# Readers of a PSUM tile in a fixed order, ScalarE alone on two kinds of shared tile, and every engine's order made anew

## The chip, the cores and the metric

The kernel runs on one core of a Trainium2 chip. The time is the device time of one launch in microseconds (us); shown is the median of several runs. The engines of the core: TensorE (PE, its weight loads are PEld), VectorE (DVE), ScalarE (ACT), GpSimd (POOL) and SyncE (SP). PE writes only into PSUM, eight banks here; DVE and ACT read PSUM and SBUF. DMA transfers are issued by SP, by POOL where they accumulate, and a few by ACT.

## The reference

The input x is 2048 x 512 in float32. One branch filters it with a two-dimensional Fourier transform, the other is a dense layer of 512 to 1792 to 512 with gelu, and a gate per row mixes them:

```python
X = jnp.fft.rfft2(x, axes=(-2, -1))
a = jnp.fft.irfft2(X * (w_r + 1j * w_i), s=(S, D), axes=(-2, -1))
h = _gelu(jnp.einsum("bsd,df->bsf", x, w1) + b1)
b = jnp.einsum("bsf,fd->bsd", h, w2) + b2
g = _sigmoid((x * gate_w).sum(-1, keepdims=True))
return g * a + (1 - g) * b
```

## The kernel before

**Arithmetic.** Products that need full precision are made of two parts per operand, a high part `h` (a copy into the fast fp32r format) and a low part `l` (the difference), and three matmuls: high by high, high by low, low by high. So nearly every result in PSUM is followed by an ACT copy (`copy`, L418) for the high part and a DVE subtraction (L460) for the low part.

**The Fourier branch.** `forward(j)` is done for 16 groups of 128 rows. PE folds the columns into two PSUM banks `pd` (one for the cosine part, one for the sine part; the gate's logit stands in two columns between). ACT copies each into the high part of `zb` (L601), DVE subtracts into its low part (L604), ACT takes the logit's two columns (L605): three reads of one PSUM tile by two engines. A second product goes to `py`: ACT copies it after its first half into `pys[0]` and again at its end into `Y[j][0]` (L622), DVE makes `pys[1]` of the two (L623), and ACT puts that into `Y[j][1]` by halves (L626). Then come radix-4 stages on DVE, the multiplication by the filter (`wf`, loaded through SP, L745 to L758), and `inverse(c, h)` eight times: products into `pz`, copied and subtracted into `zb` (L807, L808), products into `pa`; of `pa`, `od` is an ACT copy at half time, `u` an ACT copy at the end (L832), `v` = `pa` - 2 `od` on DVE (L833), and four sums and differences on DVE, two of `pa` and `u`, two of `v` (L837).

**The dense branch.** x stands in four column blocks. `CA` are the first two (done first), `CB` the last two. `seven` multiplies two blocks of x by two blocks of weights in seven products instead of eight, in the PSUM banks `nu` and `ux`; what it needs of the weights are seven tiles, `0h 0l sh sl th tl 1`, made once from `w1` for `CA` and stored to DRAM (`su<-wA..`, L1046), and loaded again for `CB` (`wB..<-su`, L406). Some tiles of `w2` go to DRAM the same way (`sb..`, L875, and `wb..b<-sb`). Other low parts come from an accumulating DMA on POOL (L403): ACT writes the negative of the high part (L465), and the DMA adds the full weight from DRAM. `gelu` works in PSUM (L878), `g_..h` is the high part of the activations (L418) and `g_..l` the low part (L460). `down` sums over four groups of rows of `w2` in `po` banks: ACT first puts the running sum `s` into the bank (L927), the matmuls add onto it, ACT takes it out again (L418).

**The end.** The blocks of `CA` leave `s` as `bacc` in DRAM (L943); the Fourier result adds it by a POOL accumulation (`w<-bacc`) and leaves by `out<-w` (L843). The blocks of `CB` are mixed in `last`: DVE makes `t` from `po` and the gate `gb` (L957), subtracts it from the Fourier result `y` (L966), and SP stores it (`out<-t`, L972; the very last piece goes by ACT, L970).

**What sets the order.** Each piece of work is a step (`add`) with an engine, a cost, a lag, and the buffers that it reads and writes. A planner, which isn't part of the file, made from these a list of step numbers, `ORDER`, and a list of buffer places, `SLOTS`. The kernel emits its steps in the order of `ORDER`, so each engine and each queue gets its instructions in that sequence and does them strictly one behind the other. Every tile has one fixed place (`slots`); where two tiles share a place, the later one waits until the earlier one's last reader is done, be it a store. These waits come from the framework, which also makes two engines take turns at one PSUM tile.

Of the kernel before, what the change touches and what calls it, by code (L numbers as in the profile page):

```python
# [16 lines left out]
P = 128  # L17
# [248 lines left out]
class Step:  # L266
    def __init__(self, n, eng, cost, lag, emit, bufs):
        self.n, self.eng, self.cost, self.lag, self.emit, self.bufs = n, eng, cost, lag, emit, bufs
        self.after = []
        self.need = 0  # L270

        self.table = None


class Graph:
# [4 lines left out]
    def add(self, eng, cost, lag, emit, reads=(), writes=()):  # L280
# [12 lines left out]
        for x in reads:  # L293
            b, ps = parts(x)
            for p in ps:
                if b.wrote[p] is not None:
                    deps.add(b.wrote[p])
# [927 lines left out]
```

## Time and profile before

| what | value |
|---|---|
| median of 3 runs | 390.59 us (389.73 to 391.59) |
| the profiled execution | 390.88 us |
| its span | 389.1 us |
| mean granted PE clock | 0.982 |
| PE busy | 362.3 us, 1782 matmuls |
| PEld busy | 299.5 us |
| DVE busy | 324.6 us, 672 instructions |
| ACT busy | 299.8 us, 614 instructions |
| POOL busy | 40.5 us |
| moved by DMA | 69.85 MB, mean 179 GB/s |

Times in the profile are us from the span's start. PE's waits are what matters most: an engine that PE never waits for may idle at no cost. SPq is SP's queue, in which transfers are issued one after the other; a transfer that waits there for its buffer holds up all behind it. A row of waits names the waiting engine, the tile it was about to write, and then what it waited for. "Granted clock" is the share of the full clock that PE got.

### The profile page before, as it was taken

What the parts mean: (1) busy time and instruction counts of PE and PEld (TensorE: products, weight loads), DVE (VectorE), ACT (ScalarE), POOL (GpSimd) and SP (SyncE); (2) the same over time, 40 slices, a digit from 0 to 9 for tenths busy, and PEclk for the clock granted to TensorE, in tenths of its full rate; (3) what the DMA queues carried; (4) which work ended last, traced back from release to release, by engine and by line L of the source; (5) the groups of instructions that cost most, each with busy time, mean ns of one, the idle gap of its engine ahead of it and who ended that gap; (6) DMA issues with size and microseconds to landing.
All of it is one profiled execution on the core that took longest, in us unless ns stands there. A gap on an engine that the chain in (4) does not pass through costs nothing. (4 is left out here: it accounts for less than half of the span.)

```text
span 389.1 us, 5714 instructions
## 1 busy us (share of the span) xinstructions
PE 362.3 (93%) x1782; PEld 299.5 (77%) x1782; DVE 324.6 (83%) x672; ACT 299.8 (77%) x614; POOL 40.5 (10%) x54
## 2 busy tenths in 40 slices
PE   7999899998897999987999999889999999999993
PEld 5977788786676788866878888668877887887882
DVE  4978698999878999969899999958789867496873
ACT  3788889889987976747867778959999998978510
POOL 1200001000104000110000002000000010111340
PEclk9899999999999999998999999989999999999997
DMA  8998385556669958795795895622123238454588
GB/s 274 326 257 288 79 219 108 141 172 210 152 205 240 275 189 259 255 224 171 223 338 151 226 293 144 144 73 71 16 54 98 91 63 266 115 89 115 135 174 259
DMA packets 46350, 69.85 MB, mean 179 GB/s; under 512 B 5488, under 2 KB 19312, under 8 KB 46320
## 3 DMA queue, kind: packets, MB, share of 16 engines
q1 hardware_dynamic: 38752, 58.36, 45.0%
q0 software_dynamic: 7136, 10.79, 18.5%
q8 instruction: 14, 0.23, 0.3%
q10 hardware_dynamic: 432, 0.33, 0.3%
q14 instruction: 16, 0.13, 0.1%
HBM read 51.76 MB, written 17.57 MB: 178 GB/s over the span
## 5 line engine op out<-in xcount | busy, mean ns | idle before, releaser
L927 ACT ACTIVATE po<-s 128x512 f32<-128x512 f32 (+1 forms) x49 | 28.6, 588 | 3.5 <-DVE t L957 3.1
L418 ACT ACTIVATE s<-po 128x512 f32<-128x512 f32 x40 | 23.4, 592 | 4.3 <-PE po L409 4.1
L788 ACT ACTIVATE sw<-y,al 64x512 f32<-64x512 f32 x32 | 23.0, 720 | 2.0 <-DVE y L654 1.5
L409 PE MATMUL py<-zb,tf 128*128 128x258 f32 x96 | 20.1, 303 | 2.9 <-ACT pys L622 2.0
L749 DVE TENSOR_TENSOR m<-y,wf 128x514 f32<-128x514 f32 x32 | 21.2, 690 | 1.1 <-ACT wf L746 0.5
L409 PE MATMUL pd<-cf,w 128*128 128x129 f32 x128 | 19.6, 280 | 1.3 <-ACT logit L605 0.6
L409 PEld LDWEIGHTS pz<-tg,pq 128*128 128x128 f32 x128 | 17.2, 190 | 3.5 <-DVE pq L795 1.6
L409 PEld LDWEIGHTS pd<-cf,w 128*128 128x128 f32 x128 | 17.5, 193 | 3.0 <-ACT logit L605 0.8
L409 PE MATMUL pz<-tg,pq 128*128 128x128 f32 x128 | 18.4, 277 | 1.1 <-DVE pq L795 0.9
L409 PEld LDWEIGHTS py<-zb,tf 128*128 128x128 f32 x96 | 14.9, 189 | 5.6 <-ACT pys L622 2.8
L409 PE MATMUL nuB<-xB,wB0h 128*128 128x512 f32 x56 | 17.7, 397 | 0.2 <-DMA wB0h<-su 0.2
L795 DVE SCALAR_TENSOR_TENSOR pq<-y,al,sw 128x256 f32<-128x256 f32 x32 | 15.2, 479 | 2.4 <-ACT sw L791 1.5
L409 PE MATMUL pa<-zb,ci 128*128 128x256 f32 x96 | 16.6, 289 | 0.6 <-DVE zb L808 0.6
L409 PEld LDWEIGHTS pa<-zb,ci 128*128 128x128 f32 x96 | 14.3, 188 | 3.4 <-DVE zb L808 1.0
L604 DVE TENSOR_TENSOR zb<-pd,zb 128x256 fp32r<-128x256 f32 x32 | 13.1, 419 | 3.5 <-ACT logit L605 2.0
L878 ACT ACTIVATE uxB<-uxB,b1t 128x512 f32<-128x512 f32 x14 | 9.1, 659 | 7.6 <-PE uxB L409 4.2
L808 DVE TENSOR_TENSOR zb<-pz,zb 128x512 fp32r<-128x512 f32 x16 | 10.8, 686 | 4.8 <-ACT zb L807 4.8
L626 ACT ACTIVATE y<-pys 64x257 f32<-64x257 f32 x32 | 13.3, 416 | 1.3 <-DVE pys L623 0.8
L409 PE MATMUL uxB<-xBt,wB 128*128 128x512 f32 x42 | 11.4, 408 | 3.0 <-DMA wB<-su 3.0
L601 ACT ACTIVATE zb<-pd 128x256 fp32r<-128x256 f32 x32 | 12.0, 389 | 2.7 <-PE pd L409 2.5
L568 DVE TENSOR_TENSOR eo<-xf 128x256 f32<-128x256 f32 x32 | 12.8, 418 | 1.2 <-DMA xf<-in_xt 1.2
L571 DVE TENSOR_TENSOR w<-eo 128x256 f32<-128x256 f32 x32 | 12.8, 420 | 0.3
(542 smaller groups left out, 1246.2 us busy)
## 6 DMA issues: line engine op xcount, KB each, us to landing
wf<-in_wf SPq DMA_DIRECT2D x16, 257.0 KB, 3.8
xf<-in_xt SPq DMA_DIRECT2D x14, 256.0 KB, 4.1
tf<-tf SPq DMA_DIRECT2D x16, 192.0 KB, 3.6
wrA<-in_w SPq DMA_DIRECT2D x10, 256.0 KB, 4.9
xbA<-in_xc SPq DMA_DIRECT2D x8, 256.0 KB
xbB<-in_xc SPq DMA_DIRECT2D x8, 256.0 KB, 6.1
bacc<-s SPq DMA_DIRECT2D x8, 256.0 KB, 4.6
w<-bacc POOLq DMA_DIRECT2D x8, 256.0 KB, 5.3
```

Of the source, the lines that this page charges most:

```text
L409: pe.matmul(ps, w, x, start=start, stop=stop, **more)
L418: a(lambda: act.activation(o.ap(), i.ap(), AF.Copy, scale=scale), n, [i], [o])
L568: v(lambda s=s, op=op: vec.tensor_tensor(eo.ap()[:, s], x.ap()[:, 0:2], x.ap()[:, 2:4], op=op), 256, [x], [(eo, s)])
L571: v(lambda s=s, op=op: vec.tensor_tensor(w.ap()[:, s], eo.ap()[:, :, 0], eo.ap()[:, :, 1], op=op), 256, [eo], [(w, s)])
L601: a(lambda c=c: act.activation(segs(xh, c), both(c), AF.Copy), 256, [ps[c]], [(xh, c)])
L604: v(lambda c=c: vec.tensor_tensor(segs(xl, c), both(c), segs(xh, c), op=ALU.subtract), 256, [ps[c], (xh, c)], [(xl, c)])
L626: a(lambda o=o, i=i: act.activation(Y[j].ap()[o:o + HP, 1], pys.ap()[i:i + HP, 1], AF.Copy), 257, [(pys, 1)], [(Y[j], 1 + k)], more=0.1)
L749: v(lambda mk=mk, k=k, y=y, w=w: vec.tensor_tensor(mk.ap(), y.ap(), w.ap()[:, k:k + 1, :ND].to_broadcast([P, 2, ND]), op=ALU.mult), 514, [ ...
L788: a(lambda sw=sw, y=y, o=o, i=i: act.activation(sw.ap()[o:o + HP], y.ap()[i:i + HP, ::-1, :HD], AF.Copy, scale=al.ap()[i:i + HP, 0:1]), 51 ...
L795: v(lambda sw=sw, pq_=pq_, y=y, j=j, k=k, op=op: vec.scalar_tensor_tensor(pq_.ap()[:, k], y.ap()[:, k, :HD], al.ap()[:, 1 + j:2 + j], sw.a ...
L808: v(lambda n=n, ps=ps: vec.tensor_tensor(zl.ap()[:, :, :, n], ps.ap(), zh.ap()[:, :, :, n], op=ALU.subtract), 512, [ps, (zh, n)], [(zl, n)])
L927: a(lambda ps=ps, n=n, o=o: act.activation(ps.ap(), o.ap()[:, n], AF.Copy), size, [o], [ps])
```

## The change

Six things change.

1. In `Graph.add` a step that reads a PSUM tile now also depends on the earlier readers of that tile, so that the planner knows the readers in a fixed order.
2. In `forward` the logit's copy comes ahead of DVE's subtraction, and no longer depends on the high part; DVE's `pys[1]` reads ACT's second copy in SBUF (`Y[j][0]`) in place of `py`.
3. In `inverse` ACT copies all of `pa` as `u` (512 columns in place of 256), and DVE makes `v` and the sums from `u`; DVE no longer reads `pa`.
4. The planner's durations for transfers change: an issue on SP counts 0.06, what moves counts on a path that all queues share (`bus`), landing 2.8 (stores 3.4), an accumulation 0.9 on POOL with 3.0 to land; some single lags become the common one.
5. The first splits of x for two of the four blocks depend on the gate's buffer, which a first small gelu writes.
6. `ORDER` and `SLOTS` are new from end to end. The steps themselves are as many as before, and PE's matmuls the same.

```diff
 ORDER = """
-0 495 15 113 23 497 496 498 499 14 16 61 62 13 24 2 26 27 65 38 19 29 37 33 3 4 66 68 5 511 34 500 501 67 512 513 503
+19 0 2 495 26 15 13 1 37 496 14 25 3 16 66 28 29 33 34 4 30 35 5 6 7 8 9 511 497 38 20 498 21 512 65 513 31 500 503 62
...
-    def add(self, eng, cost, lag, emit, reads=(), writes=()):
+    def add(self, eng, cost, lag, emit, reads=(), writes=(), bus=0.0):
...
                 if b.wrote[p] is not None:
                     deps.add(b.wrote[p])
+                if b.tag in PSUM:
+                    deps.update(b.read[p])
                 b.read[p].append(s)
...
-    def dma(emit, kb, reads, writes):
-        return add("sp", kb / 340, 2.8, emit, reads, writes)
+    def dma(emit, kb, reads, writes, lag=2.8):
+        return add("sp", 0.06, lag, emit, reads, writes, kb / 340)
+
+    def store(emit, kb, reads, writes):
+        return dma(emit, kb, reads, writes, 3.4)
...
-        return add("pool", 2.3 * kb / 340, 3.4, lambda: nc.gpsimd.dma_start(dst(), src(), accum_op=ALU.add), reads, writes)
+        return add("pool", 0.9, 3.0, lambda: nc.gpsimd.dma_start(dst(), src(), accum_op=ALU.add), reads, writes, 2.3 * kb / 340)
...
+            i = i + [gate] * (c == 0)
...
         for c in range(2):
+            a(lambda c=c: act.activation(logit.ap()[:, n, c], ps[c].ap()[:, P:P + 2], AF.Copy), 2, [ps[c]], [(logit, 2 * n + c)], more=0.1)
             v(lambda c=c: vec.tensor_tensor(segs(xl, c), both(c), segs(xh, c), op=ALU.subtract), 256, [ps[c], (xh, c)], [(xl, c)])
-            a(lambda c=c: act.activation(logit.ap()[:, n, c], ps[c].ap()[:, P:P + 2], AF.Copy), 2, [ps[c], (xh, c)], [(logit, 2 * n + c)],
-              more=0.1)
...
-        v(lambda: vec.scalar_tensor_tensor(pys.ap()[:, 1], pys.ap()[:, 0], -2.0, py.ap()[:, :ND], op0=ALU.mult, op1=ALU.add), 257,
-          [py, (pys, 0)], [(pys, 1)])
+        v(lambda: vec.scalar_tensor_tensor(pys.ap()[:, 1], pys.ap()[:, 0], -2.0, Y[j].ap()[:, 0], op0=ALU.mult, op1=ALU.add), 257,
+          [(Y[j], 0), (pys, 0)], [(pys, 1)])
...
-        od, w_ = (t2k(f"{n}{c}{h}", 2 * P, cls=f"i{c}{h}") for n in ("od", "v"))
+        od, u, w_ = (t2k(f"{n}{c}{h}", 2 * P, cls=f"i{c}{h}") for n in ("od", "u", "v"))
...
-        u = t2k(f"u{c}{h}", P, cls=f"i{c}{h}")
-        a(lambda: act.activation(u.ap(), ps.ap()[:, 1], AF.Copy), 256, [ps], [u])
-        v(lambda: vec.scalar_tensor_tensor(w_.ap(), od.ap(), -2.0, ps.ap(), op0=ALU.mult, op1=ALU.add), 512, [ps, od], [w_])
+        copy(u, ps)
+        v(lambda: vec.scalar_tensor_tensor(w_.ap(), od.ap(), -2.0, u.ap(), op0=ALU.mult, op1=ALU.add), 512, [u, od], [w_])
...
-            for i, (x, z) in enumerate(((ps, lambda: u.ap().rearrange("p a b -> p (a b)")), (w_, lambda: w_.ap()[:, 1]))):
-                v(lambda w=w, op=op, i=i, x=x, z=z: vec.tensor_tensor(w.ap()[:, i, :2 * P], x.ap()[:, 0], z(), op=op), 256,
-                  [x, w_ if i else u], [(w, i)])
+            for i, x in enumerate((u, w_)):
+                v(lambda w=w, op=op, i=i, x=x: vec.tensor_tensor(w.ap()[:, i, :2 * P], x.ap()[:, 0], x.ap()[:, 1], op=op), 256,
+                  [x], [(w, i)])
```

The order moves at three places that matter below (line numbers of the changed kernel are four or five higher). First, SP's queue in the part that loads the last tiles of `wB` (`su` is their DRAM copy, `bacc` the store of a partial sum, `wb..b` tiles of `w2`, `tg` a small table). Before:

```order
L406 DMA wBsh_2739<-su_861 128x512
L851 DMA wb0l_raw<-in_w 128x512
L406 DMA wb13hb<-sb13h 128x512
L781 DMA tg_2848<-ti 128x128
L943 DMA bacc_2868<-s_1002 128x512
L406 DMA wB_2906<-su_861 128x512
L781 DMA tg_2909<-ti 128x128
L406 DMA wb12hb<-sb12h 128x512
L943 DMA bacc_2984<-s_1189 128x512
```

Now the load of the same tile, `wB_2720`, with what follows it:

```order
L947 DMA bacc_2644<-s_828 128x512
L855 DMA wb3l_raw<-in_w 128x512
L750 DMA wf_2671<-in_wf 128x2x257
L750 DMA wf_2674<-in_wf 128x2x257
L411 DMA wB_2720<-su_940 128x512
L947 DMA bacc_2740<-s_1186 128x512
L1026 DMA wrB_2742<-in_w 128x512
L411 DMA wBsh_2748<-su_940 128x512
```

The load `wB` of this group of weights was the last of its seven, right behind a store of a partial sum; it now stands ahead of the last three of the seven, of which `wBsh` is shown, and behind two filter tiles and a load of `w2` that follow a store of a partial sum.

Second, ACT around the activations `g_10h`, whose buffer the store `su<-wA0l` reads (`s` running sums, `po` the banks of `down`, `nuA`, `uxA` banks of `seven`, `xBt` and `xB` sums of x blocks). Before:

```order
L418 ACTIVATE s_900<-po_010_1688 128x512
L927 ACTIVATE po_010_2047<-s_900 128x512 [waits Activation_49]
L418 ACTIVATE g_9h<-uxA_1908 128x512 [waits DMAHW0_49,PE_49]
L878 ACTIVATE nuA_1935<-nuA_1935,b1t 128x512 [waits PE_49]
L418 ACTIVATE g_10h<-nuA_1935 128x512 [waits DMAHW6_49,DMASW3_49,Activation_49]
L418 ACTIVATE fiveA_2089<-nuA_2082 128x512 [waits DVE_49,PE_49]
L976 ACTIVATE xBt_2091<-xbB_1663 128x512 [waits DVE_49]
L852 ACTIVATE wb11h<-wb11l_raw 128x512 [waits DMAHW7_49]
L927 ACTIVATE po_000_2104<-s_939 128x512 [waits DVE_49]
```

Now:

```order
L882 ACTIVATE nuA_1903<-nuA_1903,b1t 128x512
L980 ACTIVATE xB_2016<-xbB_2005 128x512 [waits DMAHW6_49]
L470 ACTIVATE wb8l<-wb8h 128x512 [waits Activation_49]
L470 ACTIVATE wb9l<-wb9h 128x512
L423 ACTIVATE g_10h<-nuA_1903 128x512 [waits DMAHW1_49,DMASW3_49,Activation_49]
L423 ACTIVATE s_1064<-po_130_1734 128x512 [waits PE_49]
L423 ACTIVATE s_1186<-po_100_1811 128x512 [waits PE_49]
L882 ACTIVATE nuA_1976<-nuA_1976,b1t 128x512 [waits DVE_49]
```

`g_10h` came right behind its gelu, and a `po` preload four rows after it; now three copies stand between the gelu and `g_10h`, and two running sums are taken out after it.

Third, at the end of DVE's list the mixing of a block, `t`, waits for an earlier store out of the same place. Before:

```order
L957 SCALAR_TENSOR_TENSOR t_4180<-gb,po_330_4051 128x256 [waits PE_49]
L966 TENSOR_TENSOR t_4180<-y,t_4180 128x256 [waits DVE_49]
L957 SCALAR_TENSOR_TENSOR t_4205<-gb,po_320_4155 128x512 [waits DMAHW2_49,PE_49]
L966 TENSOR_TENSOR t_4205<-y,t_4205 128x512 [waits DVE_49]
L957 SCALAR_TENSOR_TENSOR t_4208<-gb,po_33256_4190 128x128 [waits PE_49]
```

Now:

```order
L961 SCALAR_TENSOR_TENSOR t_4169<-gb,po_300_4078 128x512 [waits PE_49,Activation_49]
L970 TENSOR_TENSOR t_4169<-y,t_4169 128x512 [waits DVE_49]
L961 SCALAR_TENSOR_TENSOR t_4180<-gb,po_320_4050 128x512 [waits DMAHW1_49,PE_49]
L970 TENSOR_TENSOR t_4180<-y,t_4180 128x512 [waits DVE_49]
L961 SCALAR_TENSOR_TENSOR t_4189<-gb,po_310_4161 128x512 [waits PE_49]
L970 TENSOR_TENSOR t_4189<-y,t_4189 128x512 [waits DVE_49]
L961 SCALAR_TENSOR_TENSOR t_4209<-gb,po_33256_4192 128x128 [waits PE_49]
```

The wait for a transfer (DMAHW) before the last full block is still there, now two blocks ahead of the last piece in place of one, and for another store.

More of the change, by code (lines that the diff above doesn't have):

```diff
@@ L266, with __init__ @@
 class Step:
-    def __init__(self, n, eng, cost, lag, emit, bufs):
-        self.n, self.eng, self.cost, self.lag, self.emit, self.bufs = n, eng, cost, lag, emit, bufs
+    def __init__(self, n, eng, cost, lag, emit, bufs, bus):
+        self.n, self.eng, self.cost, self.lag, self.emit, self.bufs, self.bus = n, eng, cost, lag, emit, bufs, bus
         self.after = []
@@ L278, in __init__ @@
         self.steps = []
-    def add(self, eng, cost, lag, emit, reads=(), writes=()):
-        s = Step(len(self.steps), eng, cost, lag, emit, [])
+    def add(self, eng, cost, lag, emit, reads=(), writes=(), bus=0.0):
+        s = Step(len(self.steps), eng, cost, lag, emit, [], bus)
         deps = set()
@@ L495, in tile_kernel @@
     for k in range(2):
-        add("act", 0.4, 2.4 + 0.35 * k, lambda k=k: act.dma_start(x0.ap()[:, 2 * k:2 * k + 2].rearrange("p a b -> p (a b)"),
-                                                       x0g[:, k * HD:(k + 1) * HD]), [], [(x0, k)])
-        add("sp", 128 / 340, 1.5 + 0.05 * k, lambda k=k: sp.dma_start(x4.ap()[:, 2 * k:2 * k + 2], xt[4][:, 2 * k:2 * k + 2]), [], [(x4, k)])
+        add("act", 0.4, 2.6, lambda k=k: act.dma_start(x0.ap()[:, 2 * k:2 * k + 2].rearrange("p a b -> p (a b)"),
+                                                       x0g[:, k * HD:(k + 1) * HD]), [], [(x0, k)], 128 / 340)
+        dma(lambda k=k: sp.dma_start(x4.ap()[:, 2 * k:2 * k + 2], xt[4][:, 2 * k:2 * k + 2]), 128, [], [(x4, k)])
     for j in NORD[2:4]:
@@ L629, in forward @@
                 o = j % 4 * 2 + k
-                add("sp", 0.1, 2.4, lambda k=k, o=o: sp.dma_start(own.ap()[o * 8:o * 8 + 8, :ND], yy.ap()[0:P:HP, j % 4::4, k]),
+                add("sp", 0.06, 2.8, lambda k=k, o=o: sp.dma_start(own.ap()[o * 8:o * 8 + 8, :ND], yy.ap()[0:P:HP, j % 4::4, k]),
                     [Y[i] for i in range(j % 4, NJ, 4)], [(own, o)])
@@ L646, in back @@
                 sp.dma_start(yy.ap()[k * HP:k * HP + 1], r.ap()[k * R // 2:(k + 1) * R // 2, 0])
-        add("sp", 0.4, 3.0, back, [r], Y)
+        add("sp", 0.15, 4.0, back, [r], Y, 0.3)
     def fma(o, x, s, b, n, reads, writes):
@@ L842, in inverse @@
                     256, part_of, [w])
-                dma(lambda w=w, k=k: sp.dma_start(
+                store(lambda w=w, k=k: sp.dma_start(
                     out[c][:, 2 * k:2 * k + 2, 2 * h:2 * h + 2].rearrange("p a b c -> p a (b c)"), w.ap()), 256, [w], [])
@@ L863, in load_w @@
                 o = slice(k * HD, (k + 1) * HD)
-                add("sp", 128 / 340, 1.0 + 0.25 * k, lambda o=o: sp.dma_start(t.ap()[:, o], src[:, o]), [], [(t, k)])
+                dma(lambda o=o: sp.dma_start(t.ap()[:, o], src[:, o]), 128, [], [(t, k)])
                 v(lambda o=o: vec.tensor_copy(h.ap()[:, o], t.ap()[:, o]), 256, [(t, k)], [(h, k)])
@@ L874, in load_w @@
             for k, b in zip("hl", (h, l)):
-                dma(lambda k=k, b=b: sp.dma_start(ws[f, k].ap(), b.ap().bitcast(F32)), 256, [b], [ws[f, k]])
+                store(lambda k=k, b=b: sp.dma_start(ws[f, k].ap(), b.ap().bitcast(F32)), 256, [b], [ws[f, k]])
     def gelu(ps, f):
@@ L942, in down @@
                     v(lambda o=o: vec.scalar_tensor_tensor(o.ap(), gb.ap()[:, c], 1.0, o.ap(), op0=ALU.subtract, op1=ALU.mult), 512, [gb], [o])
-                    dma(lambda o=o, q=q: sp.dma_start(bacc[c].ap()[:, q].rearrange("p a b -> p (a b)"), o.ap()), 256, [o],
+                    store(lambda o=o, q=q: sp.dma_start(bacc[c].ap()[:, q].rearrange("p a b -> p (a b)"), o.ap()), 256, [o],
                         [(bacc[c], 2 * q), (bacc[c], 2 * q + 1)])
@@ L969, in last @@
             if k:
-                add("act", 0.4, 2.6, lambda s=s, i=i, w=w: act.dma_start(dst[:, n.start + i:n.start + i + w], t.ap()[:, s]), o, [])
+                add("act", 0.4, 2.6, lambda s=s, i=i, w=w: act.dma_start(dst[:, n.start + i:n.start + i + w], t.ap()[:, s]), o, [], w / 680)
             else:
-                dma(lambda s=s, i=i, w=w: sp.dma_start(dst[:, n.start + i:n.start + i + w], t.ap()[:, s]), w / 2, o, [])
+                store(lambda s=s, i=i, w=w: sp.dma_start(dst[:, n.start + i:n.start + i + w], t.ap()[:, s]), w / 2, o, [])
     def put(b, e, x):
@@ L1045, in spread_w @@
                 for i, n in enumerate(TS):
-                    dma(lambda i=i, n=n: sp.dma_start(wu[u].ap()[:, i], T[n].ap().bitcast(F32)), 256, [T[n]], [(wu[u], i)])
+                    store(lambda i=i, n=n: sp.dma_start(wu[u].ap()[:, i], T[n].ap().bitcast(F32)), 256, [T[n]], [(wu[u], i)])
         def form(b, k):
@@ L1135, in tile_kernel @@
     a(lambda: act.activation(logit.ap()[:, 0, 0, 0:1], gate.ap()[:, 0:1], AF.Gelu_apprx_tanh), 1, [gate], [(logit, 0)]).table = "gelu"
-    dma(lambda: sp.dma_start(gsc.ap(), gate.ap()), 8, [gate], [gsc])
+    store(lambda: sp.dma_start(gsc.ap(), gate.ap()), 8, [gate], [gsc])
     for p0 in range(0, P, 32):
         gt = buf("w", [P, 32, NJ], F32, f"gt{p0}", cls="gt")
-        add("sp", 700 / 340, 6.5, lambda gt=gt, p0=p0: sp.dma_start(
+        add("sp", 0.06, 5.0, lambda gt=gt, p0=p0: sp.dma_start(
             gt.ap(), bass.AP(tensor=gsc.ap().tensor, offset=gsc.ap().offset + p0 * NJ, ap=[[0, P], [1, 32 * NJ]])),
-            [gsc], [gt])
+            [gsc], [gt], 700 / 340)
         def spread(gt=gt, p0=p0):
```

196 rows, old and new, of tables (ORDER, SLOTS) are left out of this document.

## The prediction

> **What bounds the kernel now.** I read four views, from the coarse to the fine. The page first: busy time of each engine over the span.
>
> ```profile
> span 389.1 us, 5714 instructions
> PE 362.3 (93%) x1782; PEld 299.5 (77%) x1782; DVE 324.6 (83%) x672; ACT 299.8 (77%) x614; POOL 40.5 (10%) x54
> ```
>
> TensorE (PE) is busy for 93% of the span, so a gain must come out of its idle time or its slow clock. Second, busy time per stretch of 20 us (columns: stretch, length, then busy us and instructions of PE, PEld, DVE, ACT and POOL, granted clock, DMA share, GB/s):
>
> ```profile
> 120.00:140.00 20.00, 17.66 (x76) 13.69 (x76) 17.93 (x35) 15.81 (x33) 3.13 (x4) 1.00 1.03 283
> 160.00:180.00 20.00, 16.70 (x69) 13.40 (x68) 16.15 (x30) 12.42 (x24) 2.60 (x3) 0.92 0.75 200
> 220.00:240.00 20.00, 20.00 (x90) 16.57 (x89) 19.57 (x37) 14.31 (x25) 1.47 (x2) 1.00 0.82 253
> 240.00:260.00 20.00, 17.00 (x68) 13.61 (x68) 15.57 (x33) 14.45 (x26) 2.83 (x4) 0.91 0.55 112
> 300.00:320.00 20.00, 19.40 (x112) 16.64 (x112) 15.36 (x34) 19.57 (x34) 1.31 (x2) 1.00 0.36 91
> ```
>
> A stretch without trouble, 220 to 240, holds 90 matmuls: 20/90 = 0.222 us each. The stretches from 160 and from 240 hold 69 and 68, at a mean clock of 0.92 and 0.91: two holes. Third, what PE waited for (us in total, times, longest):
>
> ```profile
> PE po L409 <- ACT po L927: 6.3, 5, 3.3
> PE uxB L409 <- DMA wB<-su: 3.0, 1, 3.0
> PE py L409 <- ACT pys L622: 2.0, 2, 1.7
> PE py L409 <- ACT logit L605: 0.9, 2, 0.5
> PE pd L409 <- ACT logit L605: 0.6, 1, 0.6
> PE pd L409 <- ACT y L622: 0.6, 1, 0.6
> ```
>
> The two holes are the 3.3 and the 3.0. Fourth, the timeline around each. The first, at 177.2 us (start, length, engine, line, operation, in brackets the wait before it), with the landing time of the `su` store:
>
> ```profile
> 165.25 1.31 POOL L403 DMA_DIRECT2D wb10l<-in_w  x1
> 166.04 0.40 SPq L1046 DMA_DIRECT2D su<-wA0l  x1
> 174.53 0.60 ACT L418 ACTIVATE g_10h<-nuA 128x512 fp32r<-128x512 f32 x1 [4.47 <-DMA su<-wA0l]
> DMA to landing us min/median/max: 8.2/8.2/8.2
> ```
>
> `g_10h` goes into a buffer that the store `su<-wA0l` still has to read. The store was issued right behind accumulating loads on GpSimd's queue and took 8.2 us to land (174.2); ScalarE stood 4.47 us in front of `g_10h`, and the preload of `po` that PE needed was four ScalarE instructions behind it. The second hole is on SyncE's queue:
>
> ```profile
> 245.10 0.32 SPq L943 DMA_DIRECT2D bacc<-s  x1
> 251.59 0.32 SPq L406 DMA_DIRECT2D wB<-su  x1
> SPq L406 <- DMA bacc<-s: 8.4, 2, 6.1
> ```
>
> The load `wB<-su` waits 6.1 us in the queue for the store of a partial sum issued just before it, since it is loaded over that store's buffer, and PE stands 3.0 us for it. After both holes the clock is low:
>
> ```profile
> 176.00:178.00 2.00, 0.80 (x2) 0.71 (x3) 2.00 (x5) 2.00 (x5) 0.00 (x0) 0.71 0.25 91
> 178.00:180.00 2.00, 2.00 (x6) 1.52 (x6) 2.00 (x5) 1.56 (x4) 0.00 (x0) 0.50 0.90 279
> 254.50:257.00 2.50, 2.46 (x8) 1.99 (x9) 0.00 (x0) 0.21 (x1) 0.00 (x0) 0.67 0.18 68
> 257.00:260.00 3.00, 3.00 (x11) 2.42 (x10) 1.88 (x5) 2.97 (x6) 0.00 (x0) 0.71 0.00 0
> ```
>
> The clock loss is busy time times the missing share: 0.80 x 0.29 + 2.00 x 0.50 = 1.2 us for the first, 2.46 x 0.33 + 3.00 x 0.29 = 1.7 us for the second. The holes cost 4.5 and 4.7 us. [...] Last, the end:
>
> ```profile
> 382.08 0.28 PE L409 MATMUL po<-g_7h,wb7l 128*128 128x256 f32 x1
> 383.39 0.69 DVE L957 SCALAR_TENSOR_TENSOR t<-gb,po 128x512 f32<-128x512 f32 x1 [2.34 <-DMA out<-t]
> ```
>
> PE is done at 382.4; VectorE (DVE) still waits 2.34 us for an output store to free the buffer of `t`, and has the last two tiles to finish behind it. The span ends 6.7 us after PE.
>
> **The change, part by part.** The sum is made against the profiled execution: 390.88 us around a span of 389.1, next to the median of 390.59.
>
> *Order.* The new table decides most. For each transfer that a later instruction waits for, I counted the matmuls that the program places between its issue and that instruction, and multiplied by 0.222. Before, `g_10h` has 14 matmuls (3.1 us) after the issue of `su<-wA0l`, against 8.2 us of landing; now it has 32 (7.1 us). Before, the product that uses `wB<-su` has 17 (3.8 us); now this load stands ahead of the accumulator stores that follow it on SyncE, and its product comes far later. So both holes go: -4.5 and -4.7. Bounds: the first leaves between 8.2 - 7.1 = 1.1 us and nothing, the second nothing.
>
> *New holes.* Past the first third, the order before has 16 waits with under 4.2 us of matmuls ahead of them, the small `tg` tables apart. Four of those or of their neighbours stalled PE, two large (3.3, 3.0) and two small:
>
> ```profile
> PE uxB L409 <- DMA wBsl<-su: 0.4, 1, 0.4
> PE nuB L409 <- DMA wB0h<-su: 0.2, 1, 0.2
> ```
>
> The new order has 6, the nearest a `wB` load with 18 matmuls (4.0 us). At the same rate that is 6 x 4/16 = 1.5 stalls of (4.5 + 4.7 + 0.4 + 0.2)/4 = 2.5 us: +3.7. Bounds 0 (none) and 6 x 2.5 = 15.
>
> *The end.* The waiting DVE step now has some 30 matmuls (6.7 us) between the store and itself where it had 16 (3.6 us): -2.3 by the 2.34 above. Bounds 0 and -2.3.
>
> *PSUM readers.* The rule orders two readers of one PSUM tile in the planner. It adds no wait on the chip: there they wait for each other already, and the wait just came unplanned. These groups show it (busy us, mean ns | idle us before, by releaser):
>
> ```profile
> L605 ACT ACTIVATE logit<-pd 128x2 f32<-128x2 f32 x32 | 5.2, 180 | 2.9 <-DVE zb L604 2.8
> L604 DVE TENSOR_TENSOR zb<-pd,zb 128x256 fp32r<-128x256 f32 x32 | 13.1, 419 | 3.5 <-ACT logit L605 2.0 <-ACT zb L601 1.5
> L623 DVE SCALAR_TENSOR_TENSOR pys<-pys,py 128x257 f32<-128x257 f32 x16 | 6.7, 416 | 2.7 <-ACT y L622 2.5
> L832 ACT ACTIVATE u<-pa 128x256 f32<-128x256 f32 x8 | 3.0, 381 | 6.4 <-DVE v L833 4.7 <-DMA out<-w 1.6
> L418 ACT ACTIVATE od<-pa 128x512 f32<-128x512 f32 x8 | 4.8, 596 | 3.1 <-PE pa L409 3.0
> L833 DVE SCALAR_TENSOR_TENSOR v<-od,pa 128x512 f32<-128x512 f32 x8 | 5.5, 686 | 6.4 <-PE pa L409 3.8 <-ACT u L832 2.4
> ```
>
> ScalarE waits for VectorE at `logit` and at `u`, VectorE for ScalarE at `zb`, `pys` and `v`. What of it reached PE are the four rows above on `pys`, `logit` and `y`: 2.0 + 0.9 + 0.6 + 0.6 = 4.1 us. ScalarE now frees `py` alone, and where ten of the 32 `logit` copies carried a wait for VectorE none does now; but `py` still waits for a ScalarE that may be elsewhere; I take half, -2.0, with bounds 0 and -4.1.
>
> *Wider copy.* `u` grows from 256 to 512 columns: 596 - 381 = 215 ns, 8 times, 1.7 us of ScalarE. All lie from 299 us on, where ScalarE is busy 19.57 of 20 us at first while PE has 19.40. What hides it is the 4.7 us in which ScalarE stood before `u` for VectorE, a wait that is gone with VectorE's read of `pa`. So 0; without that cover, +1.7.
>
> *VectorE from SBUF.* 16 `pys`, 8 `v` and 16 `w` operations read SBUF where they read PSUM. The same operation on both sources:
>
> ```profile
> L942 DVE SCALAR_TENSOR_TENSOR s<-gb,s 128x512 f32<-128x512 f32 x8 | 5.5, 684 | 0.0
> L837 DVE TENSOR_TENSOR w<-v 128x256 f32<-128x256 f32 x8 | 3.3, 418 | 0.1
> L837 DVE TENSOR_TENSOR w<-pa,u 128x256 f32<-128x256 f32 x8 | 3.3, 418 | 0.0
> ```
>
> 684 against 686, 418 against 418: 0. [...]
>
> *Planner durations* issue nothing themselves. The first loads, the filler matmuls and the gate's place shift the head by an amount that I take as 0, with bounds of -1.1 and +1.1 from the head's longest wait:
>
> ```profile
> PE none L409 <- DVE zero L477: 1.1, 1, 1.1
> ```
>
> Sum: 390.9 - 4.5 - 4.7 + 3.7 - 2.3 - 2.0 = **381.1 us**. The likeliest case alone: 375 to 387.
>
> **The rivals.**
>
> *All of it comes good*: no new hole, all 4.1 us of the readers' waits: 390.9 - 4.5 - 4.7 - 2.3 - 4.1 = 375.3, and 372.3 if the rest of the `po` row, 6.3 - 3.3 = 3.0, goes too. For it: six tight waits instead of sixteen. Against: each was absent from the plan before as well. Chance 0.19.
>
> *ScalarE becomes the bound from 300 on.* For: its 19.57 of 20 us. Its 1.7 us of `u` and what the fixed order makes it wait would come on top, with the readers' gain lost: 381.1 + 1.7 + 2.0 = 384.8. Against: the 4.7 us of idle time. Chance 0.07.
>
> *A knot stays.* In 120 to 140 PE lost 2.3 us, for the same kind of reason as at 177:
>
> ```profile
> ACT g_4h L418 <- DMA su<-wA0l: 2.1, 1, 2.1
> PE po L409 <- ACT po L927: 2.3, 2, 2.0
> ```
>
> In the new order a ScalarE copy after the row exchange waits for a store (`sb12h`) three SyncE rows behind that exchange, with a `po` preload seven ScalarE instructions later. If that store lands as late as the 8.2 us above, PE loses a hole like the first, 4.5 instead of 2.3 or so, and the rows behind the same queue one more: 381.1 + 2.2 + 4.5 = 387.8, and up to 390. Chance 0.10.
>
> *SyncE's queue runs late: slower.* The planner now counts 0.06 us for an issue on SyncE; the rows above show 0.32 to 0.40 each, up to 6.1 where the head of the queue waits. Between 220 and 340 us the new order issues seven loads per product, 7 x 0.32 = 2.2 us that the plan does not have, against the 4.0 us ahead of the tightest load. If that makes holes like the second (4.7), the sum without the 3.7 is 377.4: the third brings 391.5, the fourth 396.2. It decides from the fourth hole. For it: the second hole before was a queue held up. Against: the loads of `wB` kinds stand earlier in the new queue. Chance 0.09 for three, 0.13 for four or more.
>
> *The rule and the copy do nothing, only the new order counts*: the 2.0 is missing: 383.1, inside the forecast's own range. [...]
>
> **How the numbers follow.** Forecast 0.42, all good 0.19, ScalarE 0.07, knot 0.10, three holes 0.09, four or more 0.13. 0.5% of the time, about what a measurement of this kernel tells from no change, is 2 us: under 388.6 is faster. Faster: the first three with the lower half of the knot and less a spill of 0.01: 0.42 + 0.19 + 0.07 + 0.05 - 0.01 = 0.72. Same: half of the knot, most of the three holes: 0.11. Slower: 0.17. The range leaves out the best part of "all good" and most of four holes: 370 to 393.
>
> **What would show it.** Right: no ScalarE wait on `su<-wA0l` and no PE wait on `wB<-su` above 1 us; granted clock 0.99 or more from 140 to 340; DVE's last wait on `out<-t` gone and the span's end within 5 us of PE's; no ScalarE idle before `u` or `logit` released by VectorE; `u` at 596 ns, `v` at 685. Wrong: a PE wait over 2 us on a load of the `wB` kinds, with SyncE's queue held before it; ScalarE over 19.5 of 20 us with PE under 19; or a clock below 0.95 in any stretch past 20 us.

## The result, and the profile after

The changed kernel takes 364.19 us in the median (363.58 to 368.47), the kernel before 390.16 beside it: a ratio of 0.9356, 95% interval 0.9282 to 0.9429. It is 26 us faster; forecast were 381.1 us, range 370 to 393. The direction was right, the size less than half of what came, and the time lies below the range. The ratios compare undisturbed executions alone, those of a kernel with those of the kernel before run beside it, so they differ a little from the ratio of the medians.

The profiled execution, 368.47 us, is the slowest of those measured. Its page begins (busy us, share of the span, instructions):

```profile
span 366.7 us, 5730 instructions
PE 356.0 (97%) x1782; PEld 299.2 (82%) x1782; DVE 323.9 (88%) x672; ACT 296.2 (81%) x613; POOL 40.5 (11%) x54
```

The work of VectorE and ScalarE is about what it was (324.6 and 299.8 before), PE's busy time is 6.3 us less (362.3 before), and the span around them is 22.4 us shorter (389.1 before). All that PE still waited for, in the view of waits:

```profile
PE po L414 <- DMA wb9l<-in_w: 2.2, 1, 2.2
PE po L414 <- ACT po L931: 2.1, 2, 1.8
PE none L414 <- DVE zero L482: 1.1, 1, 1.1
PE py L414 <- DMA tf<-tf: 0.3, 1, 0.3
```

These four rows are 5.7 us. The same list of the kernel before, with its many rows of under one microsecond, adds up to 19.9. That gives an account of the 22.4 us. Listed PE waits: 19.9 - 5.7 = 14.2. The end after PE's last matmul: 6.7 before, 366.7 - 362.0 = 4.7 now, so 2.0. PE's busy time: 362.3 - 356.0 = 6.3. Together 22.5, so nothing is left over for shorter gaps. Of the 6.3, a faster clock explains about 1.3: PE's busy time times the missing share of the clock, added up over stretches of 2 us, is 4.6 us before and 3.3 now. The other 5.0 lie in the busy time of the same 1782 matmuls, and what they are is not shown.

Where it lies along the span is seen in the stretches of 20 us (length, busy us and instructions of PE, PEld, DVE, ACT, POOL, clock, DMA share, GB/s):

```profile
0.00:20.00 20.00, 18.95 (x124) 17.78 (x125) 15.40 (x49) 14.13 (x41) 3.43 (x14) 1.00 0.92 304
...
100.00:120.00 20.00, 18.21 (x72) 14.02 (x71) 17.05 (x32) 17.16 (x33) 2.55 (x3) 0.91 0.89 261
...
160.00:180.00 20.00, 17.81 (x71) 14.21 (x71) 16.53 (x33) 12.27 (x24) 0.00 (x0) 0.91 0.72 198
...
240.00:260.00 20.00, 20.00 (x90) 16.32 (x89) 19.10 (x41) 19.56 (x35) 4.33 (x5) 1.00 0.52 99
...
300.00:320.00 20.00, 19.91 (x122) 17.30 (x121) 15.41 (x37) 19.62 (x35) 0.85 (x1) 1.00 0.36 99
```

From 240 to 260 there were 68 matmuls at a clock of 0.91, now 90 at 1.00, though in a faster kernel the same stretch isn't the same work. The wait on `wB<-su` is gone from PE's list. Two holes are left, at 115 and at 167 us, each with a clock of 0.91 in its stretch. The first 20 us hold 124 matmuls; before they held 100, for a reason that a finer cut shows. Before:

```profile
5.00:10.00 5.00, 3.48 (x20) 2.76 (x18) 3.83 (x14) 2.81 (x6) 0.00 (x0) 0.96 1.04 381
10.00:15.00 5.00, 5.00 (x32) 5.00 (x33) 4.96 (x17) 2.94 (x10) 1.04 (x3) 0.70 1.04 306
```

After:

```profile
5.00:10.00 5.00, 5.00 (x36) 4.84 (x35) 4.97 (x20) 2.83 (x7) 0.00 (x0) 1.00 0.95 308
10.00:15.00 5.00, 5.00 (x46) 5.00 (x45) 4.96 (x14) 4.96 (x19) 0.89 (x1) 1.00 1.04 369
```

PE was idle for 1.5 of 5 us and then ran five at a clock of 0.70, which loses another 1.5 in this execution.

Last, the shared PSUM tiles (busy us, mean ns, then idle time before and who ended it):

```profile
L610 ACT ACTIVATE logit<-pd 128x2 f32<-128x2 f32 x32 | 5.6, 180 | 0.0
L611 DVE TENSOR_TENSOR zb<-pd,zb 128x256 fp32r<-128x256 f32 x32 | 13.0, 421 | 3.5 <-ACT logit L610 3.4
L628 DVE SCALAR_TENSOR_TENSOR pys<-pys,y 128x257 f32<-128x257 f32 x16 | 6.6, 423 | 1.5 <-ACT y L627 1.5
L423 ACT ACTIVATE u<-pa 128x512 f32<-128x512 f32 x8 | 4.8, 596 | 1.8 <-PE pa L414 1.5 <-DVE y L841 0.3
L837 DVE SCALAR_TENSOR_TENSOR v<-od,u 128x512 f32<-128x512 f32 x8 | 5.5, 690 | 3.4 <-ACT u L423 3.2
```

ScalarE waits for VectorE at none of them but 0.3 us, where it stood 2.8 us before `logit` and 4.7 before `u`. VectorE now waits for ScalarE, 3.4, 1.5 and 3.2 us, and no wait in PE's list comes from that.

### The profile page after: what moved, and what is told of

Read it like the earlier page. It is cut to its first block, busy times and chain, and to the rows that moved or that the text cites. A ratio compares the mean times of both kernels' runs of the same rounds, so it can differ in the third digit from the quotient of the medians.

```text
span 366.7 us, 5730 instructions
## 1 busy us (share of the span) xinstructions
PE 356.0 (97%) x1782; PEld 299.2 (82%) x1782; DVE 323.9 (88%) x672; ACT 296.2 (81%) x613; POOL 40.5 (11%) x54
## 4 chain that ended last, share of the span: by engine, by line
PE 54%; ACT 15%; issue 14%; DVE 8%; DMA 7%; POOL 1%; SPq 0%; POOLq 0%; ACTq 0%; DVEq 0%
PE po L414 24%; PE uxB L414 7%; PE ph L414 6%; PE nuB L414 6%; PE pd L414 3%; ACT sw L793 3%; PE py L414 3%; DMA wb9l<-in_w 3%; PE none L414 2%; DMA bacc<-s 1%; ACT sw L796 1%; DMA tf<-tf 1%; ACT s L423 1%; ACT po L931 1%; DMA wb4l_raw<-in_w 1%
## 5 line engine op out<-in xcount | busy, mean ns | idle before, releaser
L414 PE MATMUL py<-zb,tf 128*128 128x258 f32 x96 | 18.9, 292 | 0.3 <-DMA tf<-tf 0.3
L414 PE MATMUL pd<-cf,w 128*128 128x129 f32 x128 | 17.7, 274 | 0.0
L414 PEld LDWEIGHTS pd<-cf,w 128*128 128x128 f32 x128 | 16.5, 191 | 0.5
L941 ACT ACTIVATE s<-po,b2t 128x512 f32<-128x512 f32 x16 | 11.0, 687 | 3.9 <-PE po L414 3.8
L414 PE MATMUL nuA<-xA,wA0h 128*128 128x512 f32 x40 | 12.5, 394 | 0.0
```

What stands on the lines that cost most here:

```text
L414: pe.matmul(ps, w, x, start=start, stop=stop, **more)
L941: a(lambda o=o, ps=ps, q=q: act.activation(o.ap(), ps.ap(), AF.Identity, bias=b2t.ap()[:, q:q + 1]), 600, [b2t, ps], [o])
```

## The experiments

Two theories to begin with. **Theory O**: the new order carries the gain. **Theory C**: the edits do, since VectorE no longer reads `py` and `pa`. Each kernel below takes a known list of steps; where an edit makes a listed place impossible, the step that is needed is pulled directly ahead, and all else stays.

### Code and order apart

The first kernel has the new code in the old order, the second the old code in the new order.

```diff
 new code: logit first, pys[1] from Y[j][0], u of 512 columns
-ORDER, SLOTS of the changed kernel
+ORDER, SLOTS of the kernel before; 35 steps pulled ahead
```

> The changed code of the forward and inverse steps in the OLD order and the old buffer places; a copy that a step now needs earlier (the logit's, u, the second copy of py; 35 steps, 32 of them on ScalarE) is pulled directly ahead of it, everything else stays. Theory O (the new order carries the gain): no change within 1%, 386 to 394 us; PE's waits behind logit, pys and y partly gone (4.1 us before, 1 to 3 left), both big holes (3.3 and 3.0) still there. Theory C (the edits themselves carry it, VectorE being out of PSUM): at least half of the 26 us, 372 to 378.

391.49 us, ratio 1.0038 (1.0007 to 1.0069): no gain. That is what theory O said. PE's listed waits are 20.5 us, as many as before. Of the 4.1 us behind `logit`, `pys` and `y`, 1.7 are left, but others came in their place: `pa` waits 3.1 us for `zb`, and `uxB`, which had waited 3.0 us for `wB<-su`, now waits 2.6 for VectorE's `y`. Between ScalarE and VectorE the edit turned the waits round, as the view of waits of this kernel shows:

```profile
DVE v L837 <- ACT u L423: 13.1, 5, 4.7
DVE pys L628 <- ACT y L627: 4.4, 4, 1.5
DVE zb L611 <- ACT logit L610: 3.5, 4, 1.3
PE py L414 <- ACT pys L627: 1.7, 1, 1.7
```

```diff
 ORDER, SLOTS of the changed kernel; the 32 logit copies behind zb's subtraction, 17 VectorE steps pulled ahead
-new code
+old code: pys[1] from py, u of 256 columns, v and two sums from pa
```

> The NEW order and the new buffer places with the old code of the forward and inverse steps: the logit's copy behind VectorE's subtraction again (32 moved), VectorE reads py and pa again, u is 256 wide; 17 VectorE steps are pulled ahead so that they read a bank before it is reused. Theory O: 364 to 370 us, at most 2% over the changed kernel; ScalarE waits again for VectorE at logit and at u, some of it reaching PE. Theory C: 377 or more, with PE's waits in the first 60 us back to those of before (5.3 us lost there).

392.99 us, ratio 1.0091 (1.0057 to 1.0126): 0.9% slower than the kernel before. Here theory O fails, as C did in the first run. Neither half has any gain, both together have 26 us. What PE waits for (the first five rows):

```profile
PE pd L409 <- DVE pys L623: 4.8, 2, 2.6
PE pz L409 <- DVE w L837: 4.2, 2, 2.2
PE pz L409 <- DVE y L837: 3.9, 2, 3.3
PE nuB L409 <- DVE w L837: 2.8, 1, 2.8
PE nuA L409 <- DVE pys L623: 1.5, 1, 1.5
```

PE waits for a bank that VectorE has not yet read out. The longest, 3.3 us, in the timeline of this kernel (VectorE, and PE at its end):

```profile
304.26 0.48 DVE L795 SCALAR_TENSOR_TENSOR pq<-y,al,sw 128x256 f32<-128x256 f32 x1
304.65 0.69 DVE L654 TENSOR_TENSOR y<-d0d,d0d 128x512 f32<-128x512 f32 x1
...
305.25 0.29 DVE L782 TENSOR_TENSOR tg<-tg,gb 128x128 f32<-128x128 f32 x1
...
305.85 0.68 DVE L833 SCALAR_TENSOR_TENSOR v<-od,pa 128x512 f32<-128x512 f32 x1
306.45 0.75 DVE L837 TENSOR_TENSOR y<-pa,u 128x256 f32<-128x256 f32 x2
...
307.35 1.02 PE L409 MATMUL pz<-tg,pq 128*128 128x128 f32 x4 [3.25 <-DVE y L837]
```

VectorE has other work before it comes to `v` and the sums of `pa`, and PE's `pz`, which takes the same bank next, stands until they are done. ScalarE had made its `u` from that bank by 302.9 us, 4.4 us before `pz` could begin. In the changed kernel the bank is free when ScalarE's `u` is, and at the same place of the order `pz` follows without a wait:

```profile
290.88 0.59 ACT L423 ACTIVATE u<-pa 128x512 f32<-128x512 f32 x1
...
292.28 0.94 PE L414 MATMUL pz<-tg,pq 128*128 128x128 f32 x7
```

This gave **theory I** (interaction): the new order hands a bank on as soon as ScalarE is done with it and lets VectorE be late; each edit is worth what VectorE's lateness would cost PE in this order, and nothing in an order that doesn't use it.

### Each edit undone by itself in the new order

The first of these kernels pulls 7 VectorE steps ahead, the second 10, and what these moves cost is part of the prices below. The rule on readers in `Graph.add`, which emits nothing, is left out in all three.

```diff
-        v(..., Y[j].ap()[:, 0], ...), 257, [(Y[j], 0), (pys, 0)], [(pys, 1)])
+        v(..., py.ap()[:, :ND], ...), 257, [py, (pys, 0)], [(pys, 1)])
```

> New order, new code, but VectorE makes pys[1] from PSUM (py) again; 7 VectorE steps are pulled ahead so that py is read before its bank is reused. Theory I (interaction: the new order reuses a bank as soon as ScalarE has left it, so a late VectorE reader stops PE there): PE waits behind DVE pys of some 7.6 us, as in the kernel with all old code, plus lost clock: 364 + 8 = 372 us (369 to 375). Theory O (only the sequence counts, and the old code lost by something else): 363 to 366.

372.38 us, ratio 0.9496 (0.9415 to 0.9578). PE waits for `pys` again, its first row being:

```profile
PE pd L412 <- DVE pys L626: 4.0, 2, 2.2
```

```diff
-        copy(u, ps)
-        v(... od, -2.0, u ...), 512, [u, od], [w_])
+        a(lambda: act.activation(u.ap(), ps.ap()[:, 1], AF.Copy), 256, [ps], [u])
+        v(... od, -2.0, ps ...), 512, [ps, od], [w_])
```

and two of the four sums read `pa` and `u` again.

> New order, new code, but in the inverse ScalarE copies 256 columns as u and VectorE reads pa again for v and two of the four sums; 10 VectorE steps are pulled ahead. Theory I: PE waits behind DVE w and DVE y (line 837 of the old file) of some 10.9 us past 300 us: 364 + 11 = 375 us (371 to 379). Theory O: 362 to 366, since ScalarE even has 1.6 us less to do.

378.01 us, ratio 0.9667 (0.9588 to 0.9746), although ScalarE has less to copy. The waits for VectorE past 290 us are the same three as with all old code: `pz` behind `w` 4.2, `pz` behind `y` 3.9, `nuB` behind `w` 2.8.

```diff
 for each of the 32 banks pd, in ORDER
-  xh ... logit ... xl
+  xh ... xl, logit
```

> New order, new code, but each of the 32 logit copies stands directly behind VectorE's subtraction of the same bank again, as in the old code, so that ScalarE waits for VectorE there. Theory I: PE waits behind ACT logit of some 3 us: 364 + 3 = 367 us (365 to 369). Theory O: 363 to 365.

370.91 us, ratio 0.9474 (0.9402 to 0.9547), more than theory I expected. ScalarE stands 6.8 us before the logit copies:

```profile
ACT logit L608 <- DVE zb L609: 6.8, 12, 1.7
```

PE's rows behind `logit` are 3.2 us, about the 3 expected, but what is behind these copies in ScalarE's queue comes late too: `po` waits 1.4 us for the copy `y`, `pd` 0.8.

The changed kernel itself ran beside these three:

> The changed kernel itself, unchanged, beside the others and with a second profile. If the 4 us between its profiled execution (368.5 us, clock 0.989) and its other ones (363.6 to 364.5) are PE's slow clock behind the two holes, an execution near 364 shows the same two PE waits (1.8 and 2.2 us) with a clock of 0.995 or more. Rival: the holes themselves are shorter in the fast executions.

363.07 us, ratio 0.9284 (0.9220 to 0.9349). Against it the three edits are worth 0.0212, 0.0383 and 0.0190 of the time before: 8.3, 15.0 and 7.4 us at 390.8, together 30.7; by the intervals each is known to some 4 us. All three undone at once cost 1.0091 - 0.9284 = 0.0807, 31.5 us, between runs on two chips, each against the kernel before on its own. So they add up in this order, as far as the runs can tell. The wide copy of `u`, which I priced at 0, is the largest.

The second profile of the changed kernel comes from an execution of 361.36 us at a clock of 1.000:

```profile
PE po L414 <- DMA wb9l<-in_w: 1.2, 1, 1.2
PE none L414 <- DVE zero L482: 1.1, 1, 1.1
PE po L414 <- ACT po L931: 0.8, 1, 0.8
```

Expected were the same two holes without the slow clock; the rival was right that the holes themselves are shorter too, 1.2 and 0.8 us in place of 2.2 and 1.8. In this execution the clock is 1.00 in both stretches, in the first profile 0.91. The 7 us between the two profiled executions are both: 2.6 us of listed waits (5.7 against 3.1) and 4.4 of PE's busy time (356.0 against 351.6), of which the slow clock, added up as above, explains 3.3.

### Could the old code use the new order if VectorE hurried?

```diff
 old code, ORDER and SLOTS of the changed kernel, logit behind
-  VectorE's 16 pys, 8 v and 16 sums of pa at their listed places
+  each directly behind the last step that it needs
```

> The old code in the new order once more, but adapted by hand: each of VectorE's 40 steps that read py or pa stands directly behind the last step that it needs, so that VectorE leaves these banks as early as its queue allows; the logit copies stay behind VectorE's subtraction. Theory I (what stops PE is a bank that VectorE leaves late): PE's waits behind DVE pys, w and y fall from 18.5 us to under 8, and the time from 393 to 375 to 384 us. Rival (these steps merely take VectorE's time away from what else PE needs at that moment): the waits change their names, 387 us or more.

392.79 us, ratio 1.0107 (1.0072 to 1.0143): a miss for my expectation, and the rival is right. PE's listed waits are 25.7 us (25.4 without the hurry). VectorE leaves the banks sooner, but then stands itself in its queue until the bank is full:

```profile
DVE pys L623 <- PE py L409: 13.2, 7, 4.6
ACT logit L605 <- DVE zb L604: 9.9, 14, 1.9
DVE v L833 <- PE pa L409: 7.5, 5, 2.4
```

and what PE needs from VectorE behind them, `zb` and `g_3l`, is late instead. So here a second reader costs in either place: late it holds the bank, early it holds VectorE. Whether an order planned from the start for the old code, with the new durations and the rule on readers, would gain something was not tried.

### Holes taken away

Into the kernel before: one tile in another place.

```diff
 SLOTS, the entry of g0_10h
-31
+38
 ORDER: the load of wB0l4, which takes place 38 next, three steps later
```

> The kernel before with one activation tile (the one that waited for the store su<-wA0l) in another buffer place, and the one load that takes that place next issued three steps later; nothing else moves. By the prediction's term the hole of 3.3 us and its slow clock go: 390.2 - 4.5 = 385.7 us, and the offset between PE's time and its work stays at 21 us past 180 us in place of 26. Rival: ScalarE or the same store holds the next instruction instead, and PE waits as long: 389 to 391.

391.75 us, ratio 1.0029 (0.9992 to 1.0066): nothing, where the 4.5 us of the term would have been a ratio of 0.988. The wait on `su<-wA0l` is gone, and this stands in the view of waits from 160 to 180 us:

```profile
ACT wb11h L852 <- DMA su<-wAsh: 3.1, 1, 3.1
PE po L409 <- ACT po L927: 2.1, 1, 2.1
```

ScalarE waits three instructions on, for the next store of the same bunch, and the same `po` preload is late, 2.1 in place of 3.3 us. What was won went in the stretches that follow:

```profile
160.00:180.00 20.00, 17.92 (x78) 14.54 (x77) 18.71 (x35) 14.18 (x29) 2.60 (x3) 0.99 0.80 224
180.00:200.00 20.00, 19.50 (x80) 15.60 (x80) 15.79 (x28) 12.01 (x24) 0.86 (x1) 0.93 0.72 213
200.00:220.00 20.00, 19.01 (x83) 15.07 (x82) 18.30 (x35) 15.41 (x29) 0.86 (x1) 1.00 0.74 235
220.00:240.00 20.00, 19.38 (x86) 15.71 (x85) 19.47 (x35) 14.18 (x26) 1.70 (x2) 1.00 0.83 250
240.00:260.00 20.00, 17.82 (x76) 14.34 (x75) 16.81 (x35) 14.59 (x26) 3.45 (x4) 0.95 0.58 126
```

These are 403 matmuls in 100 us; before there were 404 (69, 89, 88, 90, 68). PE runs ahead by nine and waits for the loads and the low parts that had been in time only because of the hole.

Into the changed kernel, against its own two holes. At 115 us ScalarE stands 2.4 us before `wb6h`, a copy that the order has directly behind the issue of its own load, with the `po` preloads behind it. At 167 us PE waits for `wb9l`, an accumulating load that was issued in a bunch of three and took 10.1 us to land.

```diff
 ORDER
-  load wb6l, copy wb6h, ... po preloads
+  load wb6l, ... po preloads, copy wb6h
-  copy wb9h ... copy wb8h ... negatives of wb8l, wb9l ... accumulate wb8l ... wb9l
+  copy wb9h, negative of wb9l, accumulate wb9l ... copy wb8h, negative of wb8l, accumulate wb8l
```

> The changed kernel with two local moves: ScalarE's copy wb6h, which stood directly behind the issue of its own load, comes after three po preloads; and the negatives and the accumulating loads of wb8l and wb9l come some 15 to 40 steps earlier on ScalarE and GpSimd. If the two holes that are left in the changed kernel (PE waits of 1.8 and 2.2 us, at 115 and 167 us) are due to these, both go: 364.2 - 4.0 = 360 us, clock 0.995 or more in every execution. Rival (what follows is just as late, PE loses it a few us on): 363 to 365.

361.81 us, ratio 0.9261 (0.9225 to 0.9297), between the 360 expected and the 363 of the rival. Both holes are gone, `wb9l` lands in 5.7 us, PE is busy for 98% of the span, as it is in the second profile of the changed kernel. To see whether that is a gain over the changed kernel, both were run on one chip:

> The changed kernel once more, as the partner of the next run on the same chip: 363 to 365 us.

361.92 us, ratio 0.9303 (0.9264 to 0.9343).

> The changed kernel with both local moves, beside it: the two holes cost the changed kernel between 2.3 us (fast executions: 0.95 + 1.33) and 7 us (the profiled one, with its slow clock), so 361 to 362 us with a narrower spread. If the holes' time comes back elsewhere: 363 to 364.

362.92 us, ratio 0.9325 (0.9281 to 0.9369): no gain that can be told. The profile of this execution has one PE wait of 0.5 us and none above it past the start, yet PE is not ahead: the changed kernel beside it has 90 matmuls in each of 120 to 140 and 140 to 160 us, this one 88 and 87. VectorE is busy 19.86 of 20 us from 140 to 160 in both. In that execution of the changed kernel the two waits come to 1.0 and 0.3 us, so 1.3 us is what this pair could gain, less than it can resolve. The second move alone:

> The changed kernel with the second move alone (negatives and accumulating loads of wb8l and wb9l earlier): the landing of wb9l, 9.1 to 10.1 us in a bunch of three, falls to about 6, the PE wait at 162 to 167 us goes, the one at 114 stays; 361.5 to 363 us. Rival (the wait moves to another load of the bunch): 363 to 364.5.

362.60 us, ratio 0.9325 (0.9272 to 0.9377), with the wait for `wb9l` gone: again the same time. So two of PE's longest remaining waits are worth nothing that these runs resolve; that a full VectorE is the reason is likely, but not shown. No version here beats the changed kernel by more than the runs' uncertainty.

## Why the prediction was wrong, point by point

**What failed is the step on the readers of PSUM, and that the terms were added as if each stood by itself.** I priced the edits by the waits that they would remove from the old order: half of the 4.1 us of PE's rows, -2.0, and 0 for `u` and for VectorE's source. As waits that was not far off: in the old order 2.4 of the 4.1 us went. But others took their place, and the time gained nothing (ratio 1.0038). In the new order the edits carry 31 us, because PE in that order takes a bank again as soon as ScalarE has left it, and stands where VectorE still reads it. The trace of before could not show this price as a wait; it showed the condition for it: banks with two readers on two well filled queues, at 40 VectorE steps and 32 logit copies. I read those rows and asked what they cost, and not what an order could do without them.

**The order by itself** was the rival to which I gave 383.1: "the rule and the copy do nothing, only the new order counts". The new order with the old code takes 393.0, so that rival is out as well, for this order. What the planner's rule and the new durations each did for the order was not tested.

**The two big holes, -4.5 and -4.7.** The waits named are gone. What they were worth is another matter: `old_no_hole`, which takes the first away from the kernel before, gains nothing, because the next store and then the next loads are just as late. The term priced a wait, not the slack behind it. The second was not taken away by itself, so its 4.7 is not shown. Which of the new order's many other moves keep the changed kernel from paying the same elsewhere was not tested; the one lead that I counted (32 matmuls for 14) says nothing of the stores and loads behind it.

**New holes, +3.7.** Two came, of 1.8 and 2.2 us in the profiled execution, both with a slow clock, 0.8 and 1.2 us in another: between about 2 and 8 us with the clock. The size was fair by luck, since the place was not: of the two, one is an accumulating load, the other a copy behind its own load, and none is a `wB` load. What the runs add is that taking them out brought no gain that could be told.

**The end, -2.3.** Measured 2.0: VectorE's wait on `out<-t` is gone, and the span ends 4.7 us after PE in place of 6.7. Right.

**The head, 0 with bounds of 1.1.** Mis-sized: 1.5 us of idle PE and, between these two executions, 1.5 us of slow clock are gone between 5 and 15 us, some 3 us. The second part differs between executions: `code_old_order`, in the order before, was idle for 1.6 us from 5 to 10 and then ran at 1.00. I bounded the term by the longest single wait (1.1) and left out the sum of the short ones and the clock behind them, though I had counted just that for the big holes.

**Prices of single instructions** held. `u` takes 596 ns as expected, `v` 690 from SBUF against 686 from PSUM, `pys` 423 against 416: VectorE gains nothing per instruction from SBUF here, as the rows of before said.

**The rivals.** ScalarE did not become the bound: it is busy 19.56 to 19.62 of 20 us from 240 to 260 and from 300 to 320 and PE 20.00 and 19.91 there. The knot after the row exchange is not what stops PE at 115 us; the copy `wb6h` is: the hole stays where only the accumulating loads are moved (`fix_b_only`) and goes where the copy is moved too. SyncE's queue made no hole on a `wB` load: none stands in PE's list. "All good", 372 to 375, came nearest, and was still 8 to 11 us short, since it also took only the named rows. A cruder sum would have come nearer: all listed PE waits, 19.9, all lost clock, 7.0, and 2.0 of the end from 390.9 leave 362.0. That 7.0 is the missing share of the clock times the whole span, 0.018 x 389.1, and some 2.0 of it fall behind PE's last matmul (7.1 us at a clock of 0.72), where they cost PE nothing. That the sum comes so near is partly luck: the profile after still has 5.7 us of listed waits and 3.3 of lost clock, and its PE time is shorter by 5.0 us that this sum doesn't contain.

**The signs.** Of those named ahead, ScalarE's wait on `su<-wA0l`, PE's on `wB<-su`, VectorE's on `out<-t` and all but 0.3 us of ScalarE's waits for VectorE before `u` and `logit` are gone. A clock below 0.95 past the first 20 us was to mean that I was wrong; it came in two stretches of the first profile (0.91) and its last 6.7 us (0.90), in none of the second and in the last 20 us of the third (`after_5`, 0.91), in a kernel that is faster than forecast.

## What to carry to other kernels

When an edit and a new order come together, price the edit inside the order that will use it: ask what an early release lets the order do, since the waits of the old trace show only what the old order happened to pay. A PSUM bank with readers on two queues is a coupling of PE to both; giving it to one engine, even with a wider copy, carried 31 us here in an order that used it, and gained nothing in one that didn't (ratio 1.0038, at most 1.0069). Removing one long wait from a tightly packed order need not be a gain: look first for the next late thing behind it.

## What the runs showed of the hardware

In three executions of the changed kernel (`after`, `after_again`, `after_5`) three accumulating loads of 256 KB were issued within 1.2 us. The first, `wb8l`, landed in 6.1 us each time, the second, `wb9l`, in 10.1, 9.1 and 8.2, the third, `wb10l`, in 11.6, 10.3 and 9.7. Where `wb9l` was issued first, some 1.2 us ahead of `wb8l`, it landed in 5.7 us (`fix_ab`), 5.5 (`fix_ab_5`) and 4.7 (`fix_b_only`). Whether the place in the bunch, the spacing or other transfers made the difference is not shown.

A PE wait of about 2 us did not decide by its length whether the clock fell: 1.8 and 2.2 us went with 0.91 over 20 us in the changed kernel, 2.0 us with 1.00 in the kernel before (120 to 140 us). Behind the 1.8 us it was 0.50 from 117 to 119 us, behind the 2.2 us 0.50 from 168 to 170, and behind the 3.3 us of the kernel before 0.50 from 178 to 180. Nor did several short gaps: 1.5 of 5 us went with 0.70 over the next five in the kernel before, 1.6 of 5 us with 1.00 in `code_old_order`. So the price of a hole of this size differs by some 1.8 us (0.09 x 20) depending on whether the clock falls with it; in the two profiled executions of the changed kernel, 0.91 stands against 1.00 in just these stretches.
